# A decode layer's forward and backward pass: how the query weight is loaded at the start and again in the second half, and how the down projection's weight is cut

## The chip, the core and the metric

The kernel runs on one core of a Trainium2 chip. The core has a matrix engine (PE, with a queue of weight loads, PEld), a vector engine (DVE), a scalar engine (ACT), a general engine (POOL) and a queue that only issues transfers (SP). Transfers between the device memory and the on-chip memory of 128 partitions are issued by SP, ACT and POOL and carried by sixteen DMA engines that all three share. The metric is the time of one execution in device microseconds (us), the median of several runs.

## The reference

A layer of one token for four sequences: layer norm, attention of 32 heads over a cache of 4096 positions, output projection, a second layer norm and a gated feed-forward block. The result is the output and the gradients of everything, for a given output gradient.

```python
def _A_ref(x, k_cache, v_cache, wq, wo):            # x 4x1x512, caches 4x32x4096x128, bf16
    q = (x @ wq).reshape(B, Sq, H, Dh).transpose(0, 2, 1, 3)
    p = _softmax(jnp.einsum("bhqd,bhkd->bhqk", q, k_cache) * (Dh ** -0.5), axis=-1)
    o = jnp.einsum("bhqk,bhkd->bhqd", p, v_cache)
    return o.transpose(0, 2, 1, 3).reshape(B, Sq, H * Dh) @ wo
def _B_ref(x, w1, w3, w2):                          # F = 1792
    return (_silu(x @ w1) * (x @ w3)) @ w2
h = x + _A_ref(_layernorm(x), k_cache, v_cache, wq, wo)
out = h + _B_ref(_layernorm(h), w1, w3, w2)
# returned: out, and the gradients of x, k_cache, v_cache, wq, wo, w1, w3, w2
```

The caches and their gradients are 128 heads (4 sequences by 32) of 1 MB for each of the keys, the values, the keys' gradient and the values' gradient. The values are read twice, so five times 128 MB pass between memory and chip, beside some 34 MB of weights and their gradients.

## The kernel before

**Slots.** Most on-chip memory is 23 slots of 128 x 4160 bf16. A `Slot` (line 105) takes the number at the head of the queue `free`, makes a tile under that number's tag (line 108), and `give` (line 119) puts the number back at the queue's end. One slot holds a head of a cache, a head of a gradient, or a part of a weight.

**The order** of the instructions on each engine is the order in which the Python code makes them (`manual_schedule`, line 95); the framework adds the semaphore waits. Transfers issued by SP and by ACT share eight landing semaphores in turn, so such a transfer is issued only when the one eight places before it in that common order has landed. POOL's transfers have eight of their own.

**Start.** Lines 130 to 133 load the query weight `wq`, 512 x 4096, as four slots of 128 rows: four transfers by SP, each partition one row of 8192 bytes. After them SP loads the keys of eight heads. Lines 265 to 276 compute the layer norm, transpose the normalized rows (`rows_to_T`, line 219) and multiply by `wq`.

**First half** (loop at line 611, two heads a turn): keys are transposed, multiplied with the query, softmaxed; DVE weights the keys (line 418); PE forms a matrix M for each head (line 433), from which the output and later the query's gradient are read. One M slot holds 16 heads, eight in all. A generator `d_hh_units` (line 504) runs beside it, one piece a turn: it loads the down projection's weight with `load_w2` (line 496, two transfers of 128 rows x 7168 bytes by SP) and transposes it.

**Second half** (loop at line 1174, one head `s` a turn, 128 turns). `front(s + 1)` transposes the values on PE (line 760), copies them back on ACT (line 761) and forms the column `dP_ps` on PE (line 1147). `grad_V(s + 1)` (line 773) makes the values' gradient `gv` on DVE and stores it from POOL; `grad_K(s)` (line 1153) makes the keys' gradient `gk` on DVE and stores it from SP (line 1164). `prefetch` (line 1167) lets ACT load the values of a head seven ahead (line 793). A store frees its slot only when it has landed.

**Beside it** the generator `side_work` (line 947) runs from turn `S0` = 21 on: one step a turn until turn 58, three steps a turn from 59 on (line 1189), a step reaching to the next `yield`. It has these parts:
- 128 matmuls `dq_ps` (line 959), three a step. When the sixteenth of an M slot is done, the slot is given back; after the slots number 3 and 5 `load_wq2` (line 953) takes a slot and lets SP load 128 rows of `wq` again.
- the query's gradient `dqT_bf`, its rows into a slot `dqflat`, transferred by POOL (lines 967 to 978).
- four blocks `cc` of the gradient before the layer norm (lines 981 to 1001), nine steps each: two empty steps, four groups of eight transposes `pt_wq` on PE (line 989) with a copy on ACT (line 991), 32 matmuls `dx_ps` (line 994); then the slot is given back and block `cc + 2` is loaded.
- the weights' gradients, with 14 stores by POOL, and a second `load_w2` (line 1016).

Of the kernel before, what the change touches and what calls it, by code (L numbers as in the profile page):

```python
# [10 lines left out]
BF16 = mybir.dt.bfloat16  # L11
# [6 lines left out]
SLOT = 4160  # L18
NSLOT = 23
# [5 lines left out]
def kernel(  # L25
# [22 lines left out]
    nc = tc.nc  # L48
    P = nc.NUM_PARTITIONS

    B = A_x.shape[0]
    D = A_x.shape[-1]
    H = A_k_cache.shape[1]
    Sk = A_k_cache.shape[2]
    Dh = A_k_cache.shape[3]
    F = B_w1.shape[1]
    NH = B * H
    HD = H * Dh
    assert NH == P and Dh == P and H == 32 and Sk == 32 * P
    assert D == 4 * P and F % P == 0  # L60
    DC = D // P
    SJ = Sk // P
    FC = F // P
# [3 lines left out]
    MC = 16  # L67
# [32 lines left out]
    slotp = ctx.enter_context(tc.tile_pool(name="slotp", bufs=1))  # L100


    free = deque(range(NSLOT))

    class Slot:
        def __init__(self, name, src=free):
            self.i = src.popleft()
            self.t = slotp.tile([P, SLOT], BF16, name=name, tag=f"slot{self.i}")

        def b(self, n=4096):  # L110
            return self.t[:, 0:n]
# [16 lines left out]
    nc.gpsimd.dma_start(out=gr, in_=g2)  # L128

    wq_s = [Slot(f"wq{cc}") for cc in range(DC)]  # L130
    for cc in range(DC):
        nc.sync.dma_start(out=wq_s[cc].b(HD), in_=A_wq[cc * P:(cc + 1) * P, :])

    Ks, Vs, KTs, PKs = {}, {}, {}, {}

# [22 lines left out]
    ident_f = const.tile([P, P], FP32, name="ident_f")  # L158
# [16 lines left out]
    def ones_window(col):  # L175
# [11 lines left out]
                          in_=rowg[:, None, :, None].to_broadcast([P, 4, 8, 4]))  # L187
# [9 lines left out]
    xhatT = pers.tile([P, DC, B], BF16, name="xhatT")  # L197
# [20 lines left out]

    def rows_to_T(psA, dst, src_rows, n, nchunks):
        pt = psA.tile([P, nchunks, n], FP32, tag="rT", name="pt_rT")  # L220
        for c in range(nchunks):
            nc.tensor.transpose(pt[:, c, :], src_rows[0:n, c * P:(c + 1) * P], ident_f[0:n, 0:n])
        nc.vector.tensor_copy(out=dst, in_=pt[:])

    def layernorm_rows(xrows_ap, n, xhat_out, rstd_out):
# [32 lines left out]
    with ExitStack() as c0:  # L258
        ps0 = c0.enter_context(tc.tile_pool(name="ps0", bufs=1, space=bass.MemoryType.PSUM))
        sg = ps0.tile([G, P], FP32, name="sg_ps")  # L260
        nc.tensor.transpose(sg[:], rowg[:, 0:G], ident_f[:])
        nc.vector.tensor_scalar(out=selg[:], in0=sg[:], scalar1=-scale, scalar2=None, op0=ALU.mult)
        xh_s = Slot("xh")
        xh = xh_s.f(D)[0:B, :]
        layernorm_rows(xr, B, xh, rstd_x[:])
        nc.vector.tensor_copy(out=xhat, in_=xh)
        rows_to_T(ps0, xhatT[:], xh, B, DC)
        xh_s.give()
        qT_ps = ps0.tile([P, H, B], FP32, name="qT_ps")
        for h in range(H):  # L270
            for cc in range(DC):
                nc.tensor.matmul(qT_ps[:, h, :], lhsT=wq_s[cc].b(HD)[:, h * Dh:(h + 1) * Dh], rhs=xhatT[:, cc, :],
                                 start=(cc == 0), stop=(cc == DC - 1))
        nc.vector.tensor_copy(out=qT_bf.rearrange("d (h b) -> d h b", b=B), in_=qT_ps[:])
        for sl in wq_s:
            sl.give()
        qr_ps = ps0.tile([P, 4, NH], FP32, name="qr_ps")
        for r in range(2):
            for t_ in range(2):
                for q in range(4):  # L280
                    nc.tensor.matmul(qr_ps[32 * q:32 * (q + 1), 2 * r + t_, :], lhsT=ident_b[:, 64 * r + t_:64 * (r + 1):2],
                                     rhs=qT_bf[:], start=True, stop=True, tile_position=(0, 32 * q))
        nc.vector.tensor_copy(out=qrep[:], in_=qr_ps[:])
# [203 lines left out]
    def two_slots(nm):  # L487
        return [Slot(nm + "a"), Slot(nm + "b")]

    def w13_view(sl, cc):  # L490
        return sl[cc // 2].b(2 * F).rearrange("p (c f) -> p c f", c=2)[:, cc % 2, :]

    def w2_view(sl, fc):
        return sl[fc // 7].b(7 * D).rearrange("p (c j) -> p c j", c=7)[:, fc % 7, :]

    def load_w2():
        sl = two_slots("w2")
        for i in range(2):
            nc.sync.dma_start(out=sl[i].b(7 * D).rearrange("p (c j) -> p c j", c=7),
                              in_=B_w2.rearrange("(p c) j -> p c j", c=FC)[:, i * 7:(i + 1) * 7, :])  # L500
        return sl


    def d_hh_units():
        w2 = load_w2()
        w2T = two_slots("w2T")
        gT = fw.tile([P, DC, B], BF16, name="gT", tag="gT", bufs=1)
        yield
        yield
        pt = psX.tile([P, DC, B], FP32, tag="x", name="pt_gT")  # L510
        for c in range(DC):
            nc.tensor.transpose(pt[:, c, :], gr[0:B, c * P:(c + 1) * P], ident_f[0:B, 0:B])
        nc.vector.tensor_copy(out=gT[:], in_=pt[:])
        nc.vector.tensor_copy(out=grT[:], in_=pt[:])
        gr_s.give()
        yield
        for jj in range(DC):
            for i in range(2):
                pt = psT.tile([P, GW, P], BF16, tag="tps", name="pt_w2")
                for k in range(7):  # L520
                    nc.tensor.transpose(pt[:, k, :], w2_view(w2, 7 * i + k)[:, jj * P:(jj + 1) * P], ident_b[:])
                nc.scalar.copy(out=w13_view(w2T, jj).rearrange("q (p c) -> q p c", c=FC)[:, :, i * 7:(i + 1) * 7],
                               in_=pt[:, 0:7, :].rearrange("q c p -> q p c"))
                yield
        for sl in w2:
            sl.give()
        ps = psX.tile([P, FC, B], FP32, tag="x", name="dhh_ps")
        for fc in range(FC):
            for jj in range(DC):
                nc.tensor.matmul(ps[:, fc, :], lhsT=w13_view(w2T, jj)[:, fc * P:(fc + 1) * P], rhs=gT[:, jj, :],  # L530
                                 start=(jj == 0), stop=(jj == DC - 1))
        nc.vector.tensor_copy(out=d_hhT[:], in_=ps[:])
        for sl in w2T:
            sl.give()
# [76 lines left out]
    for gi in range(NGI):  # L611
        nxt = gi < NGI - 1
        a, na, nb = gi * G, gi * G + 2, gi * G + 3
# [182 lines left out]
    with ExitStack() as cm:  # L796
# [7 lines left out]
        pt = psA.tile([P, DC, B], FP32, tag="rT", name="pt_hT")  # L804
# [118 lines left out]
    with ExitStack() as c2:  # L923
# [23 lines left out]
        def side_work():  # L947
            pt = psg.tile([P, Dh], BF16, tag="gps", name="pt_O")
            nc.tensor.transpose(pt[:], OT_bf[:], ident_b[:])
            nc.scalar.copy(out=O_sb[:], in_=pt[:])  # L950
            wq2s = deque()

            def load_wq2(cc):
                wq2s.append(Slot("wq2"))
                nc.sync.dma_start(out=wq2s[-1].b(HD), in_=A_wq[cc * P:(cc + 1) * P, :])

            dq_ps = psx.tile([P, 512], FP32, tag="x2", name="dq_ps")
            for s in range(NH):
                nc.tensor.matmul(dq_ps[:, s:s + 1], lhsT=M_of(s)[:, 0:Dh], rhs=dOT_f[:, s:s + 1], start=True, stop=True)
                if s % MC == MC - 1:  # L960
                    Ms[s // MC].give()
                    if s // MC in (3, 5):
                        load_wq2(s // MC // 5)
                if s % 3 == 2:
                    yield
            yield
# [4 lines left out]
            pt = psg.tile([P, P], BF16, tag="gps", name="pt_dq")  # L971
# [6 lines left out]
            yield  # L978

            dx_ps = psx.tile([P, 512], FP32, tag="x2", name="dx_ps")  # L980
            for cc in range(DC):
                yield
                yield
                wq2 = wq2s.popleft()
                wv = wq2.b(HD).rearrange("p (n c) -> p n c", c=P)
                for h0 in range(0, H, 8):
                    pt = psg.tile([P, 8, P], BF16, tag="gps", name="pt_wq")
                    for i in range(8):
                        nc.tensor.transpose(pt[:, i, :], wv[:, h0 + i, :], ident_b[:])  # L989
                    yield  # L990
                    nc.scalar.copy(out=wv[:, h0:h0 + 8, :], in_=pt[:])
                yield
                for h in range(H):
                    nc.tensor.matmul(dx_ps[0:B, cc * P:(cc + 1) * P], lhsT=dqT_bf[:, h * B:(h + 1) * B], rhs=wv[:, h, :],
                                     start=(h == 0), stop=(h == H - 1))
                    if h == H // 2 - 1:
                        yield
                wq2.give()
                if cc + 2 < DC:
                    load_wq2(cc + 2)  # L1000
                yield
            yield
            fs = Slot("fin")
# [10 lines left out]
            for cc in range(DC):  # L1014
                if cc == DC - 2:
                    w2 = load_w2()
# [18 lines left out]
            for dst_rows, srcT in ((hh_rows, hhT_bf), (dg_rows, d_gateT_bf), (du_rows, d_upT_bf)):  # L1035
                for c0 in range(0, FC, 7):
                    pt = psg.tile([B, 7, P], BF16, tag="gps", name="pt_Tr")
# [5 lines left out]
            pt = psg.tile([P, FC, B], BF16, tag="gps", name="pt_hhp")  # L1043
# [15 lines left out]
            for i in range(2):  # L1059
                st = Slot("gw2")  # L1060
                hw = hh_rows[:, i * 7 * P:(i + 1) * 7 * P].rearrange("b (p k) -> b k p", k=7)
                for k in range(7):
# [4 lines left out]
                                  in_=st.b(7 * D).rearrange("p (c j) -> p c j", c=7))  # L1067
# [4 lines left out]
            for (rows, out_ap) in ((dg_rows, out_6), (du_rows, out_7)):  # L1072
                for i in range(2):
                    st = Slot("gw13")
                    nw = hhat_bf[0:B, i * 2 * P:(i + 1) * 2 * P].rearrange("b (p k) -> b k p", k=2)
                    for k in range(2):
                        for (f0_, w_) in f_chunks:
# [5 lines left out]
                                      in_=st.b(2 * F).rearrange("p (c f) -> p c f", c=2))  # L1083
                    st.give()
            r1.give()
            for h0 in range(0, H, 8):
                st = Slot("gwo")
                ow = oflat.b(HD)[0:B, h0 * P:(h0 + 8) * P].rearrange("b (p k) -> b k p", k=8)
                for k in range(8):
# [4 lines left out]
                                  in_=st.b(8 * D).rearrange("p (k j) -> p k j", k=8))  # L1094
# [128 lines left out]
```

## Time and profile before

| What | Value |
|---|---|
| median of four runs | 1725.49 us (1725.18 to 1726.69) |
| profiled execution, its own time | 1726.69 us |
| its span in the profile | 1724.7 us |
| busy: PE, DVE, ACT, POOL | 1331.9, 1252.4, 960.8, 418.2 us |
| moved by DMA | 707.86 MB, mean 410 GB/s |
| read from and written to device memory | 422.59 MB, 282.34 MB |
| `wq` loads, all eight, issue to landing, median | 19.9 us |
| `gk` stores, `gv` stores, issue to landing, median | 23.3 us, 26.9 us |

The span runs from the first to the last recorded work on the core; the execution's own time has some 2 us around it. "Busy" is the time in which an engine worked, without the instructions that only wait or issue a transfer. The time from issue to landing ends when the slowest of the DMA engines has written its share.

### The profile page before, as it was taken

The page shows a single profiled execution, that of the slowest core. Times are in us where ns is not written, and L with a number is a line of the kernel's source. Part 1 is how long each engine was busy: PE and PEld are TensorE (multiplying, and loading weights), DVE is VectorE, ACT ScalarE, POOL GpSimd, SP SyncE. Part 2 cuts the span into 40 slices and gives each one's busy share as a digit, 9 for nine tenths or more (in the row PEclk, how much of TensorE's full clock was granted, in tenths as well). Part 3 has the DMA queues.
Part 4 walks back from the last instruction along what each step waited for, and adds up shares of the span by engine and source line. Part 5 has one row for each costly group of instructions (what it writes and reads, how often), then busy time and mean ns, then how long its engine had stood idle before and what let it go on. Part 6 is the DMA issues. An engine that isn't in the chain of part 4 may idle for free. (4 is left out here: it accounts for less than half of the span.)

```text
span 1724.7 us, 44171 instructions
## 1 busy us (share of the span) xinstructions
PE 1331.9 (77%) x19124; PEld 1130.0 (66%) x19124; DVE 1252.4 (73%) x1389; ACT 960.8 (56%) x1470; POOL 418.2 (24%) x689
## 2 busy tenths in 40 slices
PE   5888888888888888887888758587678687577762
PEld 4667666777666666877778758576566566455652
DVE  5989899889998996667677666466476466555574
ACT  3555445444454444676655536356567567567752
POOL 1211232223222321231322222133132131212130
PEclk9999999999999999666555555557675556555565
DMA  9999999999999999999999999999999999999996
GB/s 398 418 418 419 419 418 419 419 416 418 414 418 407 418 405 388 381 421 423 421 423 422 423 422 424 425 417 414 403 373 422 424 420 420 397 420 413 421 413 259
DMA packets 101762, 707.86 MB, mean 410 GB/s; under 512 B 11052, under 2 KB 15288, under 8 KB 17600
## 3 DMA queue, kind: packets, MB, share of 16 engines
q1 hardware_dynamic: 63568, 432.04, 60.9%
q0 software_dynamic: 20864, 148.22, 20.6%
q10 hardware_dynamic: 17136, 124.79, 17.7%
q8 instruction: 150, 2.46, 0.5%
q14 instruction: 44, 0.36, 0.1%
HBM read 422.59 MB, written 282.34 MB: 409 GB/s over the span
## 5 line engine op out<-in xcount | busy, mean ns | idle before, releaser
L761 ACT COPY V<-pt_tps 128x1024 bf16<-128x1024 bf16 x512 | 492.9, 1015 | 219.8 <-PE pt_tps L760 179.7
L760 PE MATMUL pt_tps<-ident_b,V 128*128 128x128 bf16 x4096 | 453.3, 293 | 87.2 <-ACT V L761 83.2
L760 PEld LDWEIGHTS <-V 128*128 128x128 bf16 x4096 | 402.7, 138 | 151.3 <-issue 142.1
L766 DVE TENSOR_TENSOR gv<-P,reps 128x4096 bf16<-128x4096 bf16 x125 | 287.1, 2297 | 202.4 <-ACT reps L1128 103.0
L766 DVE TENSOR_TENSOR gk<-dS,reps 128x4096 bf16<-128x4096 bf16 x128 | 294.0, 2297 | 116.2 <-DMA out_dram<-gv 78.0
L433 PE MATMUL M_ps<-PK,Vn 128*128 128x130 bf16 x4096 | 285.3, 222 | 50.8 <-DMA Vn<-in_A_v_cache_dram 50.7
L418 DVE TENSOR_TENSOR PK<-Kn,PK 128x4096 bf16<-128x4096 bf16 x128 | 292.3, 2283 | 32.1 <-POOL PK L414 31.8
L433 PEld LDWEIGHTS <-Vn 128*128 128x128 bf16 x4096 | 252.1, 99 | 72.3 <-DMA Vn<-in_A_v_cache_dram 66.6
L325 DVE STREAM_TRANSPOSE KT<-Kn 128x512 f32<-128x512 f32 (+1 forms) x321 | 250.6, 797 | 0.3 <-issue 0.2
L320 ACT COPY KT<-pt_tps 128x1024 bf16<-128x1024 bf16 x128 | 129.5, 1012 | 190.2 <-PE pt_tps L319 147.3
L777 POOL DMA_DIRECT2D out_dram<-gv x128 | 68.3, 533 | 657.8 <-DVE dSt L1157 610.9
L1147 PE MATMUL dP_ps<-dOT_bf,V 128*128 128x1 bf16 x4096 | 150.8, 166 | 84.2 <-ACT V L761 60.0
L1147 PEld LDWEIGHTS <-V 128*128 128x128 bf16 x4096 | 140.3, 104 | 97.4 <-ACT V L761 70.7
L1137 POOL COPY P<-P_all 128x64 bf16<-128x64 bf16 x125 | 160.2, 1282 | 0.0
L331 POOL TENSOR_TENSOR W<-qrep,wmask 128x128 bf16<-128x128 bf16 x128 | 124.4, 972 | 81.7 <-PE S_ps L351 67.1
L414 POOL COPY PK<-P_all 128x64 bf16<-128x64 bf16 x128 | 32.6, 255 | 420.9 <-ACT P_all L408 417.9
L408 ACT COPY P_all<-pt_P 32x64 bf16<-32x64 bf16 x256 | 52.1, 203 | 59.3 <-PE pt_P L404 57.0
L319 PE MATMUL pt_tps<-ident_b,Kn 128*128 128x128 bf16 x1024 | 80.8, 224 | 0.0
L1128 ACT CAST reps<-rep_ps 128x512 bf16<-128x512 f32 x62 | 36.3, 586 | 77.9 <-PE rep_ps L1125 54.0
L443 PE MATMUL kP_ps<-PK,onesw 128*32 128x512 bf16 x1024 | 79.2, 386 | 0.0
L319 PEld LDWEIGHTS <-Kn 128*128 128x128 bf16 x1024 | 62.2, 100 | 25.8 <-issue 25.8
L397 ACT ACTIVATE Pn<-E,rl 128x1024 bf16<-128x1024 f32 x64 | 73.7, 1152 | 3.2 <-DVE rl L394 3.2
(239 smaller groups left out, 1287.8 us busy)
## 6 DMA issues: line engine op xcount, KB each, us to landing
Kn<-in_A_k_cache_dram SPq DMA_DIRECT2D x128, 1024.0 KB, 15.6
Vn<-in_A_v_cache_dram SPq DMA_DIRECT2D x128, 1024.0 KB, 16.0
out_dram<-gv POOLq DMA_DIRECT2D x128, 1024.0 KB, 26.9
out_dram<-gk SPq DMA_DIRECT2D x128, 1024.0 KB, 23.3
V<-in_A_v_cache_dram ACTq DMA_DIRECT2D x119, 1024.0 KB, 14.1
V<-in_A_v_cache_dram SPq DMA_DIRECT2D x9, 1024.0 KB, 18.9
wq<-in_A_wq_dram SPq DMA_DIRECT2D x8, 1024.0 KB, 19.9
out_dram<-gw POOLq DMA_DIRECT2D x6, 896.0 KB, 37.1
```

Of the source, the lines that this page charges most:

```text
L319: nc.tensor.transpose(pt[:, i, :], Kn[:, c * GW + i, :], ident_b[:])
L320: nc.scalar.copy(out=KT[:, c * GW:(c + 1) * GW, :], in_=pt[:])
L325: nc.vector.transpose(out=KT[:, c * w_:(c + n) * w_], in_=Kn[:, c * w_:(c + n) * w_])
L331: nc.gpsimd.tensor_tensor(out=W[:, hl], in0=qrep[:, :, s:s + 1].to_broadcast([P, 4, 32]), in1=wmask[:, hl, None, :].to_broadcast([P, 4, 32 ...
L418: nc.vector.tensor_tensor(out=PK[:, :, 0:Dh].rearrange("p j (r t) -> p j r t", t=2), in0=Ks[s].heads().rearrange("p j (r t) -> p j r t", t=2),
L433: nc.tensor.matmul(hold["M"][:], lhsT=Vn[:, j, :], rhs=PK[:, j, :], start=(j == 0), stop=(j == SJ - 1))
L443: nc.tensor.matmul(hold["kP"][32 * q:32 * (q + 1), :, :], lhsT=ones_window(w), rhs=PK[:, j0:j0 + 4, 0:Dh], start=(w == 0 and c == 0), stop ...
L760: nc.tensor.transpose(pt[:, i, :], v[:, g * GW + i, :], ident_b[:])
L761: nc.scalar.copy(out=v[:, g * GW:(g + 1) * GW, :], in_=pt[:])
L766: nc.vector.tensor_tensor(out=dst.rearrange("p j (r t) -> p j r t", t=2), in0=col2[:, :, None, :].to_broadcast([P, SJ, Dh // 2, 2]), in1=r ...
L1137: nc.gpsimd.tensor_copy(out=P2s[s][:], in_=P_all[:, s, :, None].to_broadcast([P, SJ, 2]))
L1147: nc.tensor.matmul(dP_ps[:, j:j + 1], lhsT=VT[:, j, :], rhs=dOT_bf[:, s:s + 1], start=True, stop=True)
```

## The change

Four things are changed.
1. All slots become slices of one tile, `arena`, so that two slots with neighbouring numbers are one stretch of memory in each partition.
2. The first load of `wq` is two transfers instead of four. A partition gets two neighbouring rows, 16384 bytes, which lie in two slots; row `256 a + 2 p + c` is in partition `p`. `rows_to_T` picks the columns of the normalized rows in the same order.
3. `load_w2` can cut its rows: the first load has four transfers, of 120, 8, 120 and 8 rows; the second load stays at two of 128.
4. The second loads of `wq` are made in the part that uses them: the first right ahead of the blocks, with four empty steps behind it, and block `cc + 1` at the start of block `cc`. None is made among the `dq_ps` matmuls.

```diff
+    arena = slotp.tile([P, NSLOT * SLOT], BF16, name="arena")
...
-            self.t = slotp.tile([P, SLOT], BF16, name=name, tag=f"slot{self.i}")
+            self.t = arena[:, self.i * SLOT:(self.i + 1) * SLOT]
...
-    for cc in range(DC):
-        nc.sync.dma_start(out=wq_s[cc].b(HD), in_=A_wq[cc * P:(cc + 1) * P, :])
+    wq_v = []
+    for a in range(0, DC, 2):
+        v = arena[:, wq_s[a].i * SLOT:wq_s[a].i * SLOT + 2 * HD].rearrange("p (c n) -> p c n", c=2)
+        nc.sync.dma_start(out=v, in_=A_wq[a * P:(a + 2) * P, :].rearrange("(p c) n -> p c n", c=2))
+        wq_v += [v[:, 0], v[:, 1]]
...
+        rows = src_rows.rearrange("b (a p c) -> b a c p", c=2, p=P)
         for c in range(nchunks):
-            nc.tensor.transpose(pt[:, c, :], src_rows[0:n, c * P:(c + 1) * P], ident_f[0:n, 0:n])
+            nc.tensor.transpose(pt[:, c, :], rows[0:n, c // 2, c % 2, :], ident_f[0:n, 0:n])
...
-    def load_w2():
+    def load_w2(cuts=(0, P)):
         sl = two_slots("w2")
         for i in range(2):
-            nc.sync.dma_start(out=sl[i].b(7 * D).rearrange("p (c j) -> p c j", c=7),
-                              in_=B_w2.rearrange("(p c) j -> p c j", c=FC)[:, i * 7:(i + 1) * 7, :])
+            for lo, hi in zip(cuts, cuts[1:]):
+                nc.sync.dma_start(out=sl[i].b(7 * D).rearrange("p (c j) -> p c j", c=7)[lo:hi],
+                                  in_=B_w2.rearrange("(p c) j -> p c j", c=FC)[lo:hi, i * 7:(i + 1) * 7, :])
...
-        w2 = load_w2()
+        w2 = load_w2((0, 120, P))
...
                     Ms[s // MC].give()
-                    if s // MC in (3, 5):
-                        load_wq2(s // MC // 5)
...
             dx_ps = psx.tile([P, 512], FP32, tag="x2", name="dx_ps")
+            load_wq2(0)
+            for _ in range(4):
+                yield
             for cc in range(DC):
+                if cc + 1 < DC:
+                    load_wq2(cc + 1)
                 yield
                 yield
                 wq2 = wq2s.popleft()
...
                 wq2.give()
-                if cc + 2 < DC:
-                    load_wq2(cc + 2)
                 yield
```

## The prediction

> **What bounds the kernel now.** I read the page's slices first: how full the sixteen DMA engines are over the span.
>
> ```profile
> DMA  9999999999999999999999999999999999999996
> GB/s 398 418 418 419 419 418 419 419 416 418 414 418 407 418 405 388 381 421 423 421 423 422 423 422 424 425 417 414 403 373 422 424 420 420 397 420 413 421 413 259
> ```
>
> The engines are full in every slice but the last, at up to 425 GB/s, so an edit pays only where DMA engines stand idle or where the transfers themselves change. Next, busy time by stretch, at the places where the rate dips and at the end.
>
> ```profile
> 1100.00:1120.00 20.00, 6.48 (x75) 6.00 (x76) 5.38 (x5) 3.86 (x4) 0.78 (x2) 0.50 1.01 425
> ...
> 1220.00:1240.00 20.00, 10.94 (x169) 9.84 (x169) 14.63 (x12) 9.64 (x12) 8.47 (x8) 0.84 0.98 383
> 1240.00:1260.00 20.00, 16.17 (x240) 14.46 (x240) 9.40 (x8) 13.98 (x16) 2.55 (x2) 0.76 0.98 400
> 1260.00:1280.00 20.00, 15.42 (x243) 13.49 (x242) 13.96 (x20) 14.48 (x16) 4.53 (x6) 0.84 1.00 381
> 1280.00:1300.00 20.00, 16.23 (x165) 11.89 (x164) 17.32 (x16) 14.53 (x20) 8.94 (x10) 0.59 0.97 380
> ```
>
> The last two columns are DMA share and GB/s. At 1100 PE, DVE and ACT nearly stop and DMA stays full: a stall of the engines costs nothing while transfers are queued. From 1220 to 1300, where the `wq` blocks are worked on, the rate is below 424; the four rows sum to 1544 GB/s against 1696, that is 7.2 us of transfer capacity.
>
> ```profile
> 1700.00:1705.00 5.00, 0.00 (x0) 0.00 (x0) 2.85 (x4) 0.00 (x0) 0.00 (x0) 0.50 1.01 421
> 1705.00:1710.00 5.00, 0.00 (x0) 0.00 (x0) 0.00 (x0) 0.00 (x0) 0.00 (x0) 0.50 0.54 226
> 1710.00:1715.00 5.00, 0.00 (x0) 0.00 (x0) 0.00 (x0) 0.00 (x0) 0.00 (x0) 0.50 0.06 26
> 1715.00:1720.00 5.00, 0.00 (x0) 0.00 (x0) 0.00 (x0) 0.00 (x0) 0.00 (x0) 0.50 0.06 26
> ```
>
> A share of 0.06 is one engine of sixteen. So the kernel ends when one late DMA engine has emptied its queue, some 14 us after the other fifteen. The trace counts each landing in sixteen parts. The last part comes 0.1 to 0.3 us after the fifteenth on average from 180 to 660 us, within 0.8 us of all the others at 722.7, then falls behind: by 6 us at 1220. By 1284 all are level again within 2.6 us, after the dip in which the others idled; then the lag grows to the end. Time is lost for good only where this late engine, too, has nothing queued.
>
> **The change part by part.**
>
> *First `wq` load.* SP's issues and the end of the wait for the weight:
>
> ```profile
> 0.74 2.08 SPq L132 DMA_DIRECT2D wq<-in_A_wq_dram  x4
> ...
> 13.28 3.49 PE L272 MATMUL qT_ps<-xhatT,wq 128*128 128x4 bf16 x125 [2.30 <-DMA wq<-in_A_wq_dram]
> ```
>
> Two issues go, 2 x 0.42 us by the median of that line. 4.19 MB land by 13.3 us either way, since the next transfers already queue behind them, and DMA is full from 20 us on. Bounds: 0.84 us gained if the issue counted, 0.6 us lost if one partition's 16384 bytes ran as two trips of 8192 (309 ns each, the trace's median packet, on the first of each transfer). I take 0. The sixteen words of the transposes' new column order are inside PE's wait, 0 too.
>
> The Trainium skill (DMA: Bandwidth & Descriptors, section "Anatomy of one DMA — SWDGE (gpsimd) path") gives each transfer some 2 us of fixed cost beside its bytes; by that estimate four transfers one after another take 17.6 us and two take 13.6, a gain of 4 us. The trace speaks against it: four are in by 13.3 us and so overlap; the sum goes by the trace.
>
> *One tile for the slots.* The numbers of instructions of each engine are the same in both kernels; only waits differ, and those I followed name old transfers. SP has five more of the instructions that only wait and ACT 35 fewer; one lasts 28 ns in the row of line 955, so forty, even if all counted, are 1.1 us. Bounds -1.1 to +1.1, value 0: DMA's queue hides them.
>
> *`w2` in 120 and 8 rows.* A transfer of 128 rows has 128 packets and sixteen landing counts, so eight packets an engine; one of 7168 bytes takes 272 ns. No transfer of 120 or 8 rows is in the trace. At best the cut takes eight packets off the late engine in each of two transfers, 16 x 0.272 = 4.4 us less; at worst it adds as many, 4.4 us more. I take 0, the nearer row being the landing counts: this load is made near 60 us, no single engine is late before 660, and at 722.7 all are level, which wipes out what one gained. Two more SP issues (0.64 us each by the row of line 499) and two more places among the eight landing semaphores lie behind full queues.
>
> By the skill (same page, section "Why a DMA increments its semaphore by 16 and not by 1") 120 rows would run on fifteen engines and 8 rows on eight, one row each: one engine is spared 16 packets and eight get two more, which would end between -4.4 and +0.5 us by where the late engine is.
>
> *The second `wq` loads.* What these cost now:
>
> ```profile
> 1017.01 1.26 SPq L955 DMA_DIRECT2D wq<-in_A_wq_dram  x1
> ...
> 1023.91 0.34 ACTq L793 DMA_DIRECT2D V<-in_A_v_cache_dram  x1
> 1024.35 0.59 ACT L1128 CAST reps<-rep_ps 128x512 bf16<-128x512 f32 x1 [17.37 <-DMA out_dram<-gk]
> ...
> DMA to landing us min/median/max: 28.6/32.6/36.9
> ...
>   DMA wq<-in_A_wq_dram: 4.0, 4
> ```
>
> The first extra transfer shifts the turn of the eight semaphores, and ACT's load of values waits 17.4 us for a `gk` store; the one at 1105 goes with a wait of 14.9. Both are removed, and both cost nothing now (the row at 1100: 425 GB/s). The last two rows are line 955's time to landing and PE's and PEld's waits for it at line 989: 4.0 us in all, since blocks 0 and 1 are loaded long ahead.
>
> After the change block 0 is asked for in turn 61, behind the store of `gk` 61 (made by DVE until 1171.3), and must wait for the landing of `gk` 58 (made by 1143.3; stores of this stretch take 30.1 us, so about 1173). It lands 32.6 us later, at 1206. It is needed six steps later, in turn 63, after the column of head 64, which PE ends at 1186.2 now and 3 us earlier without the transposes of block 0 ahead of it: 1183. PE waits 23 us there (19 to 28 by the bounds of the landing row). Behind it on PE stand the transposes of head 65, on ACT the copy of block 0 and then the next load of values, and through them DVE's next `gk`. The other three blocks are asked for nine to eleven steps ahead, as blocks 2 and 3 are now, and keep their small waits.
>
> What covers it: DVE can still make five gradients (`gv` 64 to 66, `gk` 63 and 64), 5 MB. Queued are two `wq` loads (2 MB), values (13.5 us to landing at 7.8 us a head, 1.7 MB), `gk` (30.1 us: 3.9 MB for the late engine, 1.3 MB for the first, which land 20 us earlier) and `gv` (18.7 us: 2.4 MB, some 0.9 for the first). The early engines have 11 MB, the late one 15; at 2.47 us a MB (424 GB/s), 27 and 37 us. Until the next gradient 23 us and some 9 (transposes 1, values 4, column 1, `gk` 3) pass: 32. The early engines run dry for 5 us, the late one does not, but its lead over dryness falls by as much. It then meets the dip of 1220 to 1300, which today (7.2 us) just uses up its lag, and two more loads shift semaphores in this stretch. The 2 MB moved here are already in the queues counted, and the stretch before is shorter by their 5 us: the work of the late engine as a whole is the same, and what changes the end is its idle time alone. That is bounded by -0.8 us (the DMA share of 0.97 against 1.01 in the 20 us to 1300 filled) and +16 (the 9 us from the wait's end to the next gradient with nothing queued, and the present 7.2 over again). By the nearest row, the same dip met with 5 us less lag, I take **+5 us**.
>
> Sum on the profiled execution, 1726.7 (span 1724.7 and 2.0 around it): 1726.7 + 0 + 0 + 0 + 5 = 1731.7. That execution is the slowest of the four, 1.2 above the median, so against the median I say **1730.5 us**.
>
> **Rivals** (against the median).
> - *The wait is covered*: 1725.5 (1722.1 to 1728.9). For it: the rows at 1100, a stop of 13 us with DMA full, and 37 us of work for the late engine against 32. Against: the early engines' 27 us against the same 32, and a dip that is there already.
> - *The cut `w2` load spares the engine that ends last*: 1725.5 - 4.4 = 1721.1, faster. It decides if the lag runs through from 60 us to the end. The single engine at the end speaks for it; the level landings at 722.7 against.
> - *The queues run dry in full*: the wait of PE is followed by waits for `gk` landings on ACT as at 1024, +16: 1741.5. Against: after a stop of 23 us all those stores have landed.
> - *The parts do nothing*, the program's order being the same up to the side work: as the first rival.
>
> **How the numbers follow.** Chances: forecast 0.42 (own range 1729 to 1738), covered 0.32, spared engine 0.20, run dry 0.06. A measurement of this kernel tells about 0.2%, 3.45 us. Faster 0.20, same 0.32, slower 0.48. Range 1719.5 to 1739: it reaches a little past the spared engine's 1721.1 (1.1 us for the waits) and leaves out the dry case and the tail of the others.
>
> **What would show it.** PE's wait for `wq` at its transposes: 19 to 28 us once, against 4.0 in all. ACT's waits of 17.4 and 14.9 us near 1024 and 1113 gone, with the rate there unchanged. The dip after 1190 deeper than 7.2 us of capacity, the later course the same, 14 us of one engine at the end. If that tail is shorter by about 4 us the spared engine is right; if PE waits 20 us and DMA stays above 420 GB/s, the wait is covered. I am wrong if the first 700 us differ by more than 2.

## The result, and the profile after

The changed kernel takes 1727.88 us (median of 37 runs, 1726.32 to 1732.43). The kernel before, run beside it, takes 1725.17 us (59 runs, 1721.53 to 1730.78). The ratio is 1.0018, 95% interval 1.0013 to 1.0022: 2 to 4 us slower. The profiled execution took 1727.89 us, with a span of 1726.1.

The page of the changed kernel, the span in 40 slices of 43 us; the two rows are how full the DMA engines are and what they moved:

```profile
DMA  9999999999999999999999999999999999999996
GB/s 397 363 419 419 419 418 419 418 416 418 413 419 410 418 405 387 384 420 423 424 424 423 423 424 424 425 425 409 411 387 392 425 423 414 414 417 420 419 422 276
```

DMA counts as full in every slice but the last, as before, but the second slice moves 363 GB/s where it moved 418. That is 55 x 43.2 = 2.4 MB less, 5.7 us of transfer at 418. The other differences of 5 GB/s and more are in the second half: seven slices are better than before (the 27th 425 against 417, the 29th 411 against 403, the 30th 387 against 373, the 35th 414 against 397, the 37th 420 against 413, and the last two, 422 and 276 against 413 and 259), three are worse (the 28th 409 against 414, the 31st 392 against 422, the 34th 414 against 420).

The second slice in stretches of 5 us, the changed kernel (the columns are the length of the stretch, busy time of PE, PEld, DVE, ACT and POOL, then clock, DMA share and GB/s):

```profile
60.00:65.00 5.00, 4.13 (x83) 3.48 (x81) 4.79 (x7) 1.77 (x5) 2.67 (x6) 1.00 1.02 228
65.00:70.00 5.00, 1.85 (x24) 1.16 (x20) 4.72 (x7) 2.78 (x5) 0.00 (x0) 1.00 1.01 213
70.00:75.00 5.00, 0.01 (x1) 0.01 (x1) 0.41 (x1) 0.00 (x0) 0.00 (x0) 0.50 1.00 339
75.00:80.00 5.00, 5.00 (x48) 4.36 (x48) 0.15 (x1) 1.08 (x5) 0.24 (x1) 0.50 1.01 419
```

The kernel before, the same view:

```profile
60.00:65.00 5.00, 4.12 (x83) 3.36 (x81) 4.78 (x6) 2.09 (x6) 2.68 (x6) 1.00 1.02 419
65.00:70.00 5.00, 3.51 (x54) 2.88 (x52) 4.79 (x8) 2.78 (x5) 0.00 (x0) 1.00 1.01 418
```

The share is 1.0 in both, the rate is half: the engines are not idle, their packets take longer. This is where the cut `w2` load runs. Its 256 packets of 7168 bytes take 516 ns on average, against 277 before, and the 8192-byte packets of the loads beside it (60 to 72 us) take 595 against 315. PE then runs out of values: it does 0.01 us of work from 70 to 75, as the view of waits from 60 to 80 us shows (line 438 is the matmuls that form M; total, number, longest):

```profile
PE M_ps L438 <- DMA arena<-in_A_v_cache_dram: 8.1, 1, 8.1
```

The second place is the stretch in which the second `wq` loads were. The changed kernel:

```profile
1120.00:1140.00 20.00, 15.16 (x188) 14.30 (x186) 9.61 (x8) 9.94 (x11) 3.67 (x4) 0.50 1.01 425
...
1160.00:1180.00 20.00, 8.32 (x136) 7.69 (x136) 9.70 (x9) 8.53 (x11) 5.11 (x8) 0.67 1.01 421
1180.00:1200.00 20.00, 4.00 (x60) 3.61 (x58) 10.12 (x9) 3.27 (x4) 5.56 (x6) 0.50 1.01 425
1200.00:1220.00 20.00, 16.34 (x263) 14.91 (x262) 7.73 (x7) 15.20 (x17) 0.77 (x2) 0.83 0.94 366
```

The kernel before:

```profile
1120.00:1140.00 20.00, 15.24 (x200) 14.33 (x199) 17.08 (x13) 12.74 (x14) 8.48 (x8) 0.59 1.01 411
...
1160.00:1180.00 20.00, 16.44 (x214) 15.38 (x214) 10.33 (x10) 12.91 (x15) 7.08 (x8) 0.59 1.01 403
...
1200.00:1220.00 20.00, 12.27 (x131) 11.05 (x130) 4.71 (x3) 9.88 (x12) 2.36 (x2) 0.59 1.01 417
```

Two shallow dips (411 and 403) are gone, and a deeper one (366 against 417) has come. It follows a wait of PE, which the view of waits from 1180 to 1205 us shows (line 998 is the transposes of the `wq` blocks):

```profile
PE pt_wq L998 <- DMA arena<-in_A_wq_dram: 15.3, 1, 15.3
```

PE stops from 1183.9 to 1199.2 us for block 0. While it stops the DMA engines work off what is queued (425), and only then do they run short.

The end, from 1700 us:

```profile
1705.00:1710.00 5.00, 0.00 (x0) 0.00 (x0) 0.57 (x1) 0.00 (x0) 0.00 (x0) 0.50 1.00 418
1710.00:1715.00 5.00, 0.00 (x0) 0.00 (x0) 0.00 (x0) 0.00 (x0) 0.00 (x0) 0.50 0.20 85
1715.00:1720.00 5.00, 0.00 (x0) 0.00 (x0) 0.00 (x0) 0.00 (x0) 0.00 (x0) 0.50 0.06 26
```

One engine still ends last (0.06), but the others end some 3 us later than before, where the share was 0.54 already from 1705. The tail is shorter and starts later.

Starts of `gk` in the two profiles show how the difference builds up:

| start of `gk`, us | 0 | 24 | 42 | 60 | 66 | 102 | 127 |
|---|---|---|---|---|---|---|---|
| before | 710.9 | 882.9 | 1009.9 | 1157.3 | 1200.0 | 1514.8 | 1700.6 |
| changed | 717.1 | 888.2 | 1013.0 | 1147.9 | 1213.4 | 1517.7 | 1703.3 |
| difference | +6.2 | +5.3 | +3.1 | -9.4 | +13.4 | +2.8 | +2.7 |

Six microseconds are lost in the first half, and some are made good in the second. The swing of -9.4 and +13.4 is more than the 2 MB that now pass after `gk` 60 instead of before it, which take 4.9 us at 424 GB/s. PE's stop has a part in it: in the experiments below, with the second loads alone, `gk` 60 and 66 start 17.4 us earlier and 7.8 later than before; with twelve steps, where that stop is gone, 16.5 and 6.6 us earlier. Why `gk` 60 moves by more than 4.9 us stays open.

### The profile page after: what moved, and what is told of

The parts are those of the page before. It is cut to its first block, busy times and chain, and to the rows that moved or that the text cites. A ratio compares the mean times of both kernels' runs of the same rounds, so it can differ in the third digit from the quotient of the medians.

```text
span 1726.1 us, 44122 instructions
## 1 busy us (share of the span) xinstructions
PE 1324.8 (77%) x19124; PEld 1122.8 (65%) x19124; DVE 1253.1 (73%) x1389; ACT 960.3 (56%) x1470; POOL 415.6 (24%) x689
## 5 line engine op out<-in xcount | busy, mean ns | idle before, releaser
L767 ACT COPY arena<-pt_tps 128x1024 bf16<-128x1024 bf16 x512 | 492.4, 1016 | 199.2 <-PE pt_tps L766 180.6
L766 PE MATMUL pt_tps<-ident_b,arena 128*128 128x128 bf16 x4096 | 446.9, 290 | 85.2 <-ACT arena L767 80.7
L766 PEld LDWEIGHTS <-arena 128*128 128x128 bf16 x4096 | 396.4, 136 | 149.4 <-issue 141.6
L772 DVE TENSOR_TENSOR arena<-P,arena 128x4096 bf16<-128x4096 bf16 x125 | 287.2, 2298 | 200.2 <-ACT arena L1135 107.1
L772 DVE TENSOR_TENSOR arena<-dS,arena 128x4096 bf16<-128x4096 bf16 x128 | 294.2, 2298 | 105.3 <-DMA out_dram<-arena 100.5
L438 PE MATMUL M_ps<-arena 128*128 128x130 bf16 x4096 | 286.6, 222 | 61.1 <-DMA arena<-in_A_v_cache_dram 60.8
L423 DVE TENSOR_TENSOR arena<-arena 128x4096 bf16<-128x4096 bf16 x128 | 292.4, 2285 | 36.8 <-POOL arena L419 36.8
L438 PEld LDWEIGHTS <-arena 128*128 128x128 bf16 x4096 | 253.5, 99 | 82.5 <-DMA arena<-in_A_v_cache_dram 77.0
L330 DVE STREAM_TRANSPOSE arena<-arena 128x512 f32<-128x512 f32 (+1 forms) x321 | 250.5, 797 | 0.0
L325 ACT COPY arena<-pt_tps 128x1024 bf16<-128x1024 bf16 x128 | 129.4, 1012 | 191.4 <-PE pt_tps L324 152.7
L1154 PE MATMUL dP_ps<-dOT_bf,arena 128*128 128x1 bf16 x4096 | 151.0, 166 | 84.0 <-ACT arena L767 60.7
L1154 PEld LDWEIGHTS <-arena 128*128 128x128 bf16 x4096 | 139.8, 103 | 98.0 <-ACT arena L767 73.1
L324 PE MATMUL pt_tps<-ident_b,arena 128*128 128x128 bf16 x1024 | 80.4, 223 | 0.0
L448 PE MATMUL kP_ps<-arena,onesw 128*32 128x512 bf16 x1024 | 79.5, 387 | 0.0
L324 PEld LDWEIGHTS <-arena 128*128 128x128 bf16 x1024 | 61.9, 99 | 25.7 <-issue 25.6
## 6 DMA issues: line engine op xcount, KB each, us to landing
arena<-in_A_k_cache_dram SPq DMA_DIRECT2D x128, 1024.0 KB, 16.1
```

The source lines that it names most:

```text
L324: nc.tensor.transpose(pt[:, i, :], Kn[:, c * GW + i, :], ident_b[:])
L325: nc.scalar.copy(out=KT[:, c * GW:(c + 1) * GW, :], in_=pt[:])
L330: nc.vector.transpose(out=KT[:, c * w_:(c + n) * w_], in_=Kn[:, c * w_:(c + n) * w_])
L423: nc.vector.tensor_tensor(out=PK[:, :, 0:Dh].rearrange("p j (r t) -> p j r t", t=2), in0=Ks[s].heads().rearrange("p j (r t) -> p j r t", t=2),
L438: nc.tensor.matmul(hold["M"][:], lhsT=Vn[:, j, :], rhs=PK[:, j, :], start=(j == 0), stop=(j == SJ - 1))
L448: nc.tensor.matmul(hold["kP"][32 * q:32 * (q + 1), :, :], lhsT=ones_window(w), rhs=PK[:, j0:j0 + 4, 0:Dh], start=(w == 0 and c == 0), stop ...
```

## The experiments

All ratios are to the kernel before in runs beside the experiment, with 95% intervals. "Lost near 60 us" is worked out from the trace: 13 us less the bytes started from 59 to 72 us divided by 419 GB/s, what the kernel before moves there.

| Experiment | ratio | interval | lost near 60 us | start of `gk` 0 |
|---|---|---|---|---|
| changed kernel | 1.0018 | 1.0013 to 1.0022 | 5.8 | +6.2 |
| the cut alone | 1.0042 | 1.0027 to 1.0057 | 5.5 | +6.3 |
| changed, without the cut | 0.9990 | 0.9981 to 0.9999 | 0.0 | -0.6 |
| second loads alone | 0.9992 | 0.9982 to 1.0001 | | +0.5 |
| one tile and wide rows alone | 1.0002 | 0.9991 to 1.0012 | | -0.4 |
| cut in 64 and 64 rows | 1.0040 | 1.0025 to 1.0054 | 5.3 | +7.1 |
| cut in 112 and 16 rows | 1.0028 | 1.0018 to 1.0039 | 5.3 | +7.0 |
| cut by columns | 1.0001 | 0.9989 to 1.0013 | 0.2 | +1.6 |
| one of the two transfers cut | 1.0033 | 1.0020 to 1.0046 | 3.2 | +4.8 |
| second loads in place, by POOL | 0.9997 | 0.9989 to 1.0006 | | +0.5 |
| second loads, twelve steps | 0.9983 | 0.9974 to 0.9992 | | +0.3 |
| second loads, block 0 early | 0.9985 | 0.9976 to 0.9994 | | -0.4 |
| changed, no cut, twelve steps | 0.9995 | 0.9986 to 1.0005 | | +1.4 |

### Which part costs, which part gains

**The cut alone**, in the kernel before:

```diff
-        w2 = load_w2()
+        w2 = load_w2((0, 120, P))
```

> The kernel before with only the cut of the first w2 load (120, 8, 120, 8 rows). Theory 1 (the prediction's: the cut costs nothing, the moved second wq loads cost all): ratio to before 0.9995 to 1.0010 (-1 to +2 us), the stretch 60 to 80 us as full as before (about 420 GB/s), packets of the cut transfers 272 ns. Theory 2 (the cut's own packets are slow and slow down those beside them): start of gk(0) 6 us later than before (717 against 711), 60 to 70 us near 220 GB/s, packets of 7168 bytes 500 to 540 ns; the time +4 to +6 us (1.0023 to 1.0035) if nothing gives it back, +2 to +4 if the relief of one engine at 60 us is still there at the end.

It loses 4.7 to 9.8 us; theory 1 is out. From 60 to 70 us it moves 218 and 216 GB/s, its packets take 518 ns, and `gk` 0 starts at 717.2. The time is at the upper end of what theory 2 said or above it.

**The changed kernel without the cut** (one line, the reverse of the one above):

> The changed kernel with the first w2 load whole again (128 rows). Theory 1: as the changed kernel, +3 to +6 us against before (1.0017 to 1.0035), since the cut is worth nothing. Theory 2: 4 to 6 us faster than the changed kernel, so -4 to -1 us against before (0.9977 to 0.9994), with the start of gk(0) within 1 us of before and PE still waiting 15 to 20 us for wq near 1184.

It is faster than before by 0.2 to 3.3 us, so the other three parts together gain a little and the cut turns that into a loss. PE still waits 15.3 us for `wq` blocks at its transposes.

**The second `wq` loads alone**, moved as in the change, in the kernel before:

> The kernel before with only the second wq loads moved. Theory 1: +3 to +6 us (1.0017 to 1.0035). Theory 2: -4 to 0 us (0.9977 to 1.0000), PE waiting 15 to 20 us for wq near 1184, no wait of 17 us on ACT near 1024. If this is 0 and the run without the cut is below before, the gain comes from the one tile or the wide rows.

Between 3.1 us faster and 0.2 slower. The +3 to +6 us of theory 1 are excluded, although the wait it rests on is there, in the view of waits from 1180 to 1220 us:

```profile
PE pt_wq L992 <- DMA wq<-in_A_wq_dram: 17.6, 1, 17.6
```

**One tile and the wide rows alone:**

```diff
-            self.t = slotp.tile([P, SLOT], BF16, name=name, tag=f"slot{self.i}")
+            self.t = arena[:, self.i * SLOT:(self.i + 1) * SLOT]
...
+        nc.sync.dma_start(out=v, in_=A_wq[a * P:(a + 2) * P, :].rearrange("(p c) n -> p c n", c=2))
```

> The kernel before with only the one tile for the slots and the first wq load in rows of 16384 bytes. Both theories: -1 to +1 us (0.9994 to 1.0006), PE's first matmul with wq within 0.6 us of before. A time outside that says that one of these two parts is worth something that neither theory has.

The time is as expected: no difference. The mark for PE was missed by a little: in the order of time its matmuls with `wq` go on at 14.0 us, after a wait of 3.2 us, 0.7 later than before (the mark was 0.6):

```profile
13.99 3.52 PE L277 MATMUL qT_ps<-xhatT,arena 128*128 128x4 bf16 x126 [3.17 <-DMA arena<-in_A_wq_dram]
```

### Why the cut load is slow

**64 and 64 rows** gives every engine an equal share, with as many transfers as 120 and 8:

```diff
-        w2 = load_w2()
+        w2 = load_w2((0, 64, P))
```

> The kernel before with the first w2 load cut into 64 and 64 rows: as many transfers as the 120 and 8 rows make, but every engine has the same share (each transfer sixteen landing counts, four packets an engine). Theory A (the loss comes from the uneven share: fifteen engines, or eight): packets of 7168 bytes 272 ns, 60 to 70 us at 420 GB/s, time within 1 us of before. Theory B (the loss comes from several engines writing the same group of partitions at once, since a transfer of part of the rows gives them to the engines in another way): packets of 7168 bytes 400 to 560 ns, about 5 us lost by the start of gk(0), time +4 to +7 us. By the Trainium skill (SBUF - State Buffer, section Door 1: The DMA port swizzle) 64 rows reach 8 of 16 ports, which would be half the rate.

Theory A (the uneven share) falls: the packets take 507 ns and the rate is half, in the same stretches:

```profile
60.00:65.00 5.00, 4.14 (x83) 3.39 (x81) 4.78 (x6) 2.10 (x6) 2.64 (x6) 1.00 1.01 207
65.00:70.00 5.00, 2.61 (x37) 1.97 (x35) 4.79 (x9) 2.78 (x5) 0.03 (x1) 1.00 1.03 241
```

**112 and 16 rows** (`load_w2((0, 112, P))`):

> The kernel before with the first w2 load cut into 112 and 16 rows: again an even share (seven packets and one for each engine). Theory A: 272 ns, within 1 us of before. Theory B: most packets of the 112 rows only a little slower (300 to 420 ns), since seven rows an engine spread over the groups, the sixteen of the 16 rows 700 ns or more; 1.5 to 4 us lost by gk(0), time +1 to +4 us.

Theory A falls again. Theory B has the sign, but its size for this shape was too small: the packets take 498 ns, not 300 to 420, and 7.0 us are lost by `gk` 0, not 1.5 to 4. So my picture of which rows an engine gets was wrong for this shape.

**Cut by columns**: four transfers too, but each of all 128 rows.

```diff
-        w2 = load_w2()
+        w2 = load_w2((0, 4, 7))
...
+            for lo, hi in zip(cols, cols[1:]):
+                nc.sync.dma_start(out=sl[i].b(7 * D).rearrange("p (c j) -> p c j", c=7)[:, lo:hi],
+                                  in_=B_w2.rearrange("(p c) j -> p c j", c=FC)[:, i * 7 + lo:i * 7 + hi, :])
```

> The kernel before with the first w2 load made by four transfers as well, but of 128 rows each: four and three of the seven chunks, packets of 4096 and 3072 bytes. If transfers of part of the rows are what is slow (several engines at one group of partitions): the keys' packets beside them keep 314 ns, 60 to 70 us stays near 420 GB/s, gk(0) starts within 1.5 us of before, time within 1.5 us of before. If two more transfers in this place are slow whatever their shape (semaphore turns, descriptors): some 6 us lost by gk(0) as with the cuts by rows, time +4 to +7 us.

```profile
60.00:65.00 5.00, 4.13 (x81) 3.39 (x82) 4.78 (x6) 2.02 (x6) 2.55 (x6) 1.00 1.03 407
65.00:70.00 5.00, 3.84 (x57) 3.21 (x56) 4.79 (x8) 2.86 (x6) 0.12 (x1) 1.00 1.01 419
```

407 and 419 GB/s with smaller packets (162 and 126 ns), the loads beside them at 315 ns, 0.2 us lost: the number of transfers is not the cost, the missing rows are.

**One of the two transfers cut**, the other whole:

```diff
         for i in range(2):
+            cuts = (0, P) if i else cuts
```

> The kernel before with only the first of the two w2 transfers cut (120 and 8 rows), the second whole. The three cuts by rows all lost about as much (5.3 to 5.8 us of transfer between 59 and 72 us by bytes), which a price of each cut packet and a fixed disturbance of the stream both give. Price by packet: 128 packets of about 500 ns, 2.2 to 3.5 us lost by bytes and by gk(0), time +2 to +4 us. Fixed disturbance: 5 us or more lost again, packets of the whole transfer slow too.

By bytes 3.2 us are lost, more than half of 5.5 and within what a price by packet gives; from 65 to 70 us the rate is back at 355 on average:

```profile
60.00:65.00 5.00, 4.13 (x83) 3.39 (x81) 4.79 (x7) 2.04 (x6) 2.67 (x6) 1.00 1.04 218
65.00:70.00 5.00, 2.06 (x28) 1.42 (x25) 4.79 (x7) 2.78 (x5) 0.00 (x0) 0.94 0.99 355
```

The other sign of a fixed disturbance, slow packets of the whole transfer to the end, is not there: from 67 us on, when the cut transfer is landing (its last part comes at 67.6), 7168-byte packets take 278 ns. `gk` 0 (+4.8) and the time (3.4 to 7.9 us) are higher than the price by packet said; a fixed part is not excluded.

### What the second loads do

For these the trace gives the capacity missing in each stretch: its length less the bytes started in it divided by 424 GB/s, the rate of the undisturbed second half. In us:

| | 1120 to 1180 | 1180 to 1220 | 1220 to 1320 | 1400 to 1520 | 1000 to 1700 |
|---|---|---|---|---|---|
| before | 1.6 | 0.3 | 7.2 | 3.5 | 16.1 |
| changed | 0.0 | 2.7 | 7.1 | 2.1 | 13.8 |
| changed, without the cut | -0.1 | 3.3 | 5.4 | 2.8 | 13.7 |
| second loads alone | -0.1 | 3.0 | 7.2 | 2.2 | 14.0 |
| in place, by POOL | -0.2 | 0.4 | 6.4 | 6.5 | 14.3 |
| twelve steps | -0.2 | 0.7 | 10.3 | 3.4 | 16.6 |
| block 0 early | 1.8 | 4.1 | 4.8 | 1.6 | 14.4 |
| changed, no cut, twelve steps | -0.1 | 0.6 | 7.5 | 6.7 | 18.4 |

Each row is one profiled execution. Those of the two kernels with twelve steps were 2.6 and 3.2 us slower than the medians of their kernels. From 1000 to 1700 us the other six kernels with these loads in place by SP miss 14.9 to 16.4 us.

**In place, but issued by POOL**, in the kernel before:

```diff
-                nc.sync.dma_start(out=wq2s[-1].b(HD), in_=A_wq[cc * P:(cc + 1) * P, :])
+                nc.gpsimd.dma_start(out=wq2s[-1].b(HD), in_=A_wq[cc * P:(cc + 1) * P, :])
```

> The kernel before with its second wq loads where they are, but issued by POOL, so that they take no turn among the eight landing semaphores of SP and ACT. If moving them gained because these turns went (ACT's waits of 17 and 15 us near 1024 and 1113): those waits are gone, 1120 to 1180 us at 424 GB/s instead of 412, and the time is 1 to 3 us below before (0.9983 to 0.9994). If it gained because 2 MB are loaded later, after the values and stores of that stretch: within 1 us of before, and gk(60) near 1157 us as before.

ACT's two waits are gone and so is the loss from 1120 to 1180 us (426 and 422 GB/s in the rows that had 411 and 403):

```profile
1120.00:1140.00 20.00, 15.69 (x197) 14.73 (x196) 11.16 (x11) 9.26 (x11) 5.93 (x6) 0.59 1.01 426
1160.00:1180.00 20.00, 15.56 (x237) 14.12 (x236) 10.84 (x9) 15.78 (x19) 4.76 (x7) 0.75 1.01 422
1400.00:1420.00 20.00, 12.98 (x143) 9.69 (x143) 12.76 (x13) 12.49 (x17) 6.46 (x7) 0.67 0.95 365
1460.00:1480.00 20.00, 15.55 (x184) 12.21 (x184) 7.17 (x5) 14.66 (x20) 4.57 (x9) 0.57 0.98 350
```

But two dips come later (365 and 350, where the kernel before has 418 and 420), and PE now waits 21.3 us for the third block from 1212 on, which it did for 1.7 us before. The time is the same as before within its interval. So the first reading has the waits and the rate, the second (2 MB loaded later) has its two marks, a time within 1 us and `gk` 60 at 1156.3 us. It does not tell whether the turns are worth anything at the end.

**Twelve empty steps** instead of four behind block 0's load, in the kernel with the second loads alone moved:

> The kernel before with only the second wq loads moved, and twelve empty steps instead of four behind the first of them, so that block 0 has 2.7 turns more to land. Theory: PE's wait of 17.6 us near 1184 shrinks below 3 us, and the dip of 1200 to 1220 us (363 to 371 GB/s, some 2.7 us of capacity) is filled: 0 to 3 us faster than with four steps (0.9975 to 0.9992 against before). Rival: the wait is covered, or the same idle time of DMA comes back in the later dips: the same as with four steps within 1 us.

PE's waits for `wq` at its transposes shrink from 20.3 us in all to 1.2, and 2.3 us of capacity come back from 1180 to 1220; 3.1 us go from 1220 to 1320. It is faster than before, but against the four steps nothing can be told. The rival was right about the dip: it comes with the blocks, whenever they run, and not with PE's wait.

**Block 0 loaded after the seventh M slot**, the rest as in the second loads alone:

```diff
-                    if s // MC in (3, 5):
-                        load_wq2(s // MC // 5)
+                    if s // MC == 6:
+                        load_wq2(0)
```

> The kernel before with the second wq loads moved, but block 0 loaded after the seventh M slot is given back, some 2 turns earlier than in the changed kernel. Theory: PE's wait of 17.6 us is gone, the capacity missing at 424 GB/s falls from 3.0 to below 1 us in 1180 to 1220 us, and no dip comes back in 1120 to 1180: 0.9970 to 0.9985 against before. Rival (seen with twelve empty steps: the missing capacity went from 3.0 to 0.7 us there and from 7.2 to 10.3 in 1220 to 1320): the idle time comes with the blocks, whenever they run: 0.9980 to 0.9995.

PE does not wait for `wq` at all, but ACT does for a `gk` store, in the view of waits from 1120 to 1220 us:

```profile
ACT reps L1130 <- DMA out_dram<-gk: 30.5, 2, 19.8
```

One load by SP among the `dq_ps` matmuls brings such a wait and the loss from 1120 to 1180 back (1.8 us). From 1180 to 1220 us 4.1 us are missing where the theory said below 1, although PE does not wait: both of its marks for the rate failed, and the rival's held. The ratio lies in the ranges of both.

**The changed kernel without the cut, with twelve steps** (both edits as above):

> The changed kernel without the cut and with twelve empty steps instead of four. As the kernel before with these steps alone: 0.9975 to 0.9992 against before; the one tile and the wide rows add nothing (within 0.6 us).

A little above the expected range (0.9995 against at most 0.9992; the interval reaches in), not different from before. Of the five kernels with the moved loads and no cut three have an interval below 1 (0.9983, 0.9985, 0.9990) and gain 1.7 to 2.9 us at the middle; the intervals of the other two (0.9992, 0.9995) reach 1. Which of them is best is within the noise.

## Why the prediction was right or wrong

The forecast was 1730.5 us, the measured time 1727.88: in the range, and slower, though by no more than the 0.2% that was set as no change. The working behind it does not stand: the cut was put at 0 and cost 5 to 7 us, the second loads were put at +5 and gained a little. That the number fell into the range is luck. (The lower end of that range, 1719.5, is also half a microsecond below what its own terms give, 1721.1 - 1.1.)

**First load and one tile: 0 and 0.** Right within the noise: together 0.9991 to 1.0012. The estimate of 4 us from the fixed cost of a transfer (the section it names is on transfers issued by POOL, these are issued by SP) was rightly set aside; PE starts at 14.0 us with two transfers as against 13.3 with four.

**The cut: 0, bounds of 4.4 either way. This step failed.** It counted packets, "eight packets an engine; one of 7168 bytes takes 272 ns", and took the duration as given. The number of packets was as counted (256 in both kernels); the duration was not: 516 ns. Neither bound held this, since both were built from packets moved between engines at an unchanged price, and no load of this size in the trace was of part of the rows, to support that price. The cost was 4.7 to 9.8 us alone, outside both bounds (5.5 by the bytes lost, 4.8 at the middle between the changed kernel with and without the cut). The text's own mark, first 700 us within 2, was missed by 4.

**The rival of the spared engine.** Its premise is there. The landing records fit fifteen and eight engines: a transfer of 120 rows has sixteen records and one of 8 rows nine, and the first of each comes 0.4 to 0.5 us after the issue, 16 us and more ahead of the next, so that fifteen and eight come with the data. And one engine is ahead after the cut: of the loads of 128 rows that land from 60 to 120 us the first of the sixteen parts comes 6.5 us before the last on average, against 2.3 before, and 3.9 us before the second, against 0.2. It gave nothing, as the forecast said, since the landings are set by the other engines. The mark set for it, a tail shorter by 4 us, tells nothing. From 1680 us the last part of a landing comes 15.3 us after the fifteenth in the kernel before, 11.1 in the changed one, but also 10.6 with the one tile and wide rows alone.

**The second loads: +5. This step failed too, in its sum, not in its events.** PE came to the transposes at 1183.9 (put: 1183) and waited 15.3 us for block 0 (put: 19 to 28), because the load landed 26.9 us after its issue instead of 32.6. The engines then ran short, as put. What this cost was 2.7 us of capacity from 1180 to 1220 us (0.3 before), about half of the 5. The gain was overlooked: "Both are removed, and both cost nothing now (the row at 1100: 425 GB/s)". The two waits went, as put, and the rate at 1100 stayed (424). But one row was read; those at 1120 (411) and 1160 (403) had 1.6 us missing, which went. Another 1.4 us went from 1400 to 1520, which no step had. Together 0.3 - 2.7 + 1.6 + 0.1 + 1.4 = +0.7 us in favour of the changed kernel in these four stretches. Over all of 1000 to 1700 us the changed kernel, the one without the cut and the one with the second loads alone miss 13.7 to 14.0 us, the seven with the loads in place by SP 14.9 to 16.4: some 2 us less. The loads alone measured 3.1 us faster to 0.2 slower.

That the turns of the semaphores make the loss from 1120 to 1180 is supported from three sides: it is there with loads by SP in that stretch (1.5 to 2.0 in six kernels, 0.5 in the one cut by columns), gone with loads by POOL, and back with a single one by SP. It is not settled: the kernel cut by columns has the two waits of ACT all the same (13.7 and 16.2 us) and misses only 0.5, and with twelve steps ACT waits 14.5 us for a `gk` store, until 1174.9, and nothing is missing in that stretch. That the gain in time is this was not shown: the POOL version has lost the loss and gains nothing measurable, but it has a wait of PE of 21.3 us where the kernel before has one of 1.7. That the gain comes from the 2 MB being loaded later is the rival that stays.

**So** the number came out within 3 us because a cost that was missed (+5 to +7) and a gain that was missed (about -2) replaced a cost that was put at +5. Added up, the parts alone give 3.0 us more than the 3.1 of the ratio (7.2 for the cut, -1.4 for the loads, 0.3 for the rest: 6.1), which their intervals, 1.7 to 2.6 us either way, allow.

## What to carry to other kernels

- Before a transfer is cut, ask what the cut does to the duration of a packet, not only to their number; where the trace has no transfer of that shape, the bound has to be as wide as the price is unknown. Cut by columns, with all 128 rows in each transfer, if it must be cut.
- In a kernel that is bound by transfers, the full share of the DMA engines says nothing of their rate: read GB/s in short stretches, and every one around a wait, before calling the wait free.
- Taking a wait off one engine need not recover the transfer time lost beside it: here, with PE's wait gone, the dip came later. Sum the missing capacity over the whole phase, not over the dip.

## What the runs showed of the hardware

While loads of less than 128 rows ran, from 60 to 70 us, all transfers together moved 207 to 241 GB/s against 418 and 419, and what ran beside it was slow too. With 120 and 8, 112 and 16, and 64 and 64 rows the packets of 7168 bytes took 516 to 518, 498 and 507 ns against 277, and packets of whole loads in the same 12 us 520 to 595 against 315. 1.8 MB cost 5.3 to 5.8 us more than as whole rows; the same bytes in four transfers of all rows cost 0.2 us more.

The Trainium skill has a rule that the prediction did not use (SBUF — State Buffer, section "Door 1: The DMA port swizzle"): the on-chip memory takes transfers through sixteen ports, and 64 rows reach only eight, for half the rate. The 207 and 241 GB/s of the cut in 64 rows agree. For 112 rows my estimate from that map, with equal runs of neighbouring rows for each engine, was 300 to 420 ns; the run showed 498, so which rows an engine gets in such a transfer stays open.
